# A planned attention and gated feed-forward kernel: a cast moved from GpSimd to ScalarE, a product from VectorE to GpSimd, and a new plan

## The chip, the cores and the metric

The kernel runs on one core of a Trainium2 chip. Its engines are TensorE (PE in the profile; PEld is its weight load), VectorE (DVE), ScalarE (ACT), GpSimd (POOL) and SyncE (SP, which here only issues DMAs). Each engine works through its own queue in order; semaphores tie the queues together. The metric is the device time of one execution in microseconds (us); less is better.

## The reference: what is computed

Linear attention with a sketched polynomial feature map, followed by a gated feed-forward layer. There are 4 batches of 4 heads, 1088 positions each, 32 dimensions per head, and r = 8, so that a position has 64 features.

```python
def phi(x):
    a = einsum('rd,bhsd->bhsr', S1, x)
    b = einsum('rd,bhsd->bhsr', S2, x)
    return einsum('bhsi,bhsj->bhsij', a, b)      # flattened to 64 features
q_p, k_p = phi(q), phi(k)
kv  = einsum('bhsf,bhsd->bhfd', k_p, v)
z   = sum(k_p, axis=2)
num = einsum('bhsf,bhfd->bhsd', q_p, kv)
den = einsum('bhsf,bhf->bhs', q_p, z)[..., None] + 1e-06
x   = (num / den)                                # to 4352 tokens x 128
out = (maximum(x @ w_gate, 0) * (x @ w_val)) @ w_out     # d_ff = 1536
```

## The kernel before, in words

**Tiling.** The 1088 positions of a head are laid out as 32 rows by 34 columns, four heads to 128 partitions. Columns 0 to 31 form groups of four, 128 tokens each (8 groups per batch); the last two columns of all batches are gathered into two more groups at the end. For the keys the 34 columns form nine groups of up to four (column 9a + x is in group x). An attention stage for the keys of a batch (class K) and one for the queries of a set of groups (classes Q and G) yield xT, 128 x tokens in fp16. Its consumer, class F, is a *unit* u: four blocks of 128 tokens times 128 hidden features (512 columns), in 103 units.

**Names of operations.** A unit has `g u` (gate product, L960, into a PSUM bank), `relu u` (ACT, L965, to a tile g_sb), `v u` (value product, L972), `h u` (DVE, L982: g_sb times the PSUM bank, to a tile ht; ten tiles ht are used in turn) or, for every sixth unit, `vcp u` and `hp u` (ACT copies the bank, L977, and POOL multiplies, L987), and `o u` (L994, the output product, which adds into the bank of its group; every `o` follows the `o` of the unit before). The last unit of a group has `oe` (ACT, L1002) and a store on SP (L1011). For the keys of batch b: `kt1` (transpose on DVE, L531), `ksk` (sketch, fp32 matmuls, L542), `kt2` (transpose from PSUM, L555), `z`, `zc`, `w`, `wc` (sums over positions for the denominator; L570, L578, L584, L588), `kphi b lo` (the feature products kp for groups lo onward, L599), `vc b h` (cast of half h of v from fp32 to fp16, L606), `kv` (L613) and `kve` (L620, to bz). For the queries: `qt1` (L1034), `qsk` (L735), `qt2` (L741), `bw`, `dn`, `rd`, `an` (denominator and quotient; L769, L776, L781, L801), `qphi` (features, L867), `qtr` and `qpt` (transpose on PE, L885, and copy to SBUF, L892) or `qtd` (a transposing DMA on SP, L875), `num` (L901) and `x` (to xT; L913, or L908 for the first two groups, which take a shorter way with `qaT`, `qc`, `rdx`, `rdT`). The weights arrive in fp32, in thirds `wg0` to `wo2`, and are cast by ACT (L426: wg0, wg1, wv1) or POOL (L428: wv0, wo0, wg2, wv2, wo1, wo2).

**The start.** All first loads go into SP's queue before anything else: k0 in two parts, q0 in two parts, v0 in four, then wg0, wv0, wg1, wv1, wo0, wg2, wv2, k1, wo1, wo2, q1. Until the first unit PE runs products of a zero tile (L330) that nobody reads, one stretch of them for each stretch in which the plan sees PE idle. For batch 0 the products `kv` run over head pair 0 first, which needs `vc 0 0`, then over head pair 1, which needs `vc 0 1`.

**What sets the order.** The program does not issue its operations as written. Each is put into a list with an engine, a modelled busy time and a modelled delay until others see its result (`busy + rec + LAT[engine]`), its inputs, the PSUM banks that it takes or gives up, and a due time. Due times of units are laid on a line (`T0 + u * U`, one unit every 0.65) and handed back from an operation to its inputs (`P.dues`). `P.run` then simulates the engines: it takes the operation that could start earliest, and among those of the same engine that could start within 0.2 of it (or half its own busy time, if that is less) the one with the earliest due time. Loads of the start have no queue in this model; a table `LAND` says when each has landed. The simulated start times are used for one thing alone: all operations are issued in their order, so that they fix the order of every engine's queue and of SP's loads and stores. On the chip an engine waits at the head of its queue for whatever is not ready.

`kphi 0 8`, the features of the ninth group of columns of batch 0, is on DVE before the change (list `own`), with a DVE transpose into a PSUM bank ahead of it (`kt2b`, L563), from which it reads one of its two factors. `vc 0 1` is on POOL; every other `vc` is on ACT.

Of the kernel before, what the change touches and what calls it, by code (L numbers as in the profile page):

```python
# [35 lines left out]
class Plan:  # L36


    HOLD = 2.0
    LAT = {"PE": 0.20, "DVE": 0.035, "ACT": 0.035, "POOL": 0.06, "SP": 0.0, "DMA": 0.05}  # L40

# [105 lines left out]
def kernel(  # L147
# [12 lines left out]
    nc = tc.nc  # L160

    B, H, S, D = q.shape
# [31 lines left out]
    wv = sb([DM, DF], FP16, "wv")  # L194
# [204 lines left out]
    def act(cols):  # L399
        return cols / 1200.0 + 0.062  # L400

    def pool(cols):
        return cols * 0.00188 + 0.07

    LAND = {"k0a": 3.6, "S": 4.3, "k0b": 4.25, "q0a": 5.4, "q0b": 7.35, "v0": 9.95, "wg0": 10.35,
            "wv0": 10.99, "wg1": 11.63, "wv1": 12.27, "wo0": 12.91, "wg2": 14.75, "wv2": 15.39,
            "k1": 16.75, "wo1": 17.39, "wo2": 18.03, "q1": 19.39}
    land = {n: P.landed(n, t) for n, t in LAND.items()}
# [43 lines left out]
    class K:  # L452


        def __init__(self, b, prev):
# [27 lines left out]
            self.lz = lz  # L483
            self.z_op = P.add("PE", f"z {b}", 0.40, self.z, self.t2s, take=[lz])
            self.zc_op = P.add("DVE", f"zc {b}", 0.12, self.zc, [self.z_op], drop=[lz], rec=0.07)
# [5 lines left out]
            cut = [(0, 2), (2, 4), (4, 6), (6, KX)] if b else [(0, 2), (2, 4), (4, 6), (6, 8), (8, KX)]  # L491
            own = [4] if b == 0 else []
            lb = Lease()
            self.lb = lb
            for n, (lo, hi) in enumerate(cut):
# [11 lines left out]
                else:  # L507
                    phis.append(P.add("POOL", f"kphi {b} {lo}", pool(cols),
                                      lambda lo=lo, hi=hi: self.phi(nc.gpsimd, lo, hi), dep))
            vc = [P.add(e, f"vc {b} {h}", 0.66 if e == "POOL" else 0.58,  # L510
                        lambda h=h, e=e: self.vc(h, e), [land[f"v{b}"]],
                        rec=0.0 if e == "POOL" else 0.13)
                  for h, e in enumerate(["ACT", "ACT" if b else "POOL"])]
            lm = Lease()
# [88 lines left out]

        def vc(self, h, e):
            o, i = (t[self.b][:, 2 * h:2 * h + 2] for t in (v16, v32))
            nc.scalar.copy(out=o, in_=i) if e == "ACT" else nc.gpsimd.tensor_copy(out=o, in_=i)  # L606

# [30 lines left out]
    class Q:  # L638
# [3 lines left out]
        def __init__(self, b, x0, n, i, ks, qt1, old):  # L642
# [26 lines left out]
            else:  # L669
                self.l4 = [Lease(2), Lease(2)]  # L670
                s1 = P.add("PE", f"qsk {name}", cols / 600.0 + 0.34 + 0.37 * (n > NX),
                           self.sk, qt1 + wcs + [wq_op], take=self.l4)
                t2, t2c = [P.add("DVE", f"qt2 {name} {i}", dve(2 * cols), lambda i=i: self.t2(i),
# [12 lines left out]
            if first:  # L686

                rx = P.add("ACT", f"rdx {name}", act(256), self.rdx, [o3], rec=0.13)
                lr = Lease()
                self.lr = lr  # L690
                rt = P.add("PE", f"rdT {name}", 0.52, self.rdT, [rx], take=[lr])
                self.rdc = P.add("ACT", f"rdTe {name}", act(256), self.rdTe, [rt], drop=[lr],
                                 rec=0.13)
                self.o4 = t2
            else:
                self.o4 = P.add(e, f"an {name}", small(x * R), lambda: self.div(eng), [o3] + old,
                                rec=0.07)
            self.t2_op = t2
# [216 lines left out]
    class F:  # L915


        def __init__(self, u, grp, qg, js, prev, old):
# [13 lines left out]
                      due=t + 0.35)  # L932
            vv = P.add("PE", f"v {u}", cost, self.v, [qg.x_op, wcast[f"wv{third}"]], take=[lv], rec=0.07,
                       due=t + 0.2)
            if self.pool:
                a2 = P.add("ACT", f"vcp {u}", act(cols), self.vcp, [vv], drop=[lv], rec=0.13,
                           due=t + 0.6)
# [165 lines left out]
    P.ops = order  # L1103
    P.dues(slack)
    end = P.run()
    if __name__ != "kernel":
# [44 lines left out]
```

## Time and profile before

| | |
|---|---|
| median of 3 runs | 100.52 us (100.48 to 100.69) |
| the profiled execution | 100.48 us |
| its span, first to last instruction | 98.7 us, 3036 instructions |
| busy: PE, PEld | 94.1 us (95%), 61.6 us (62%) |
| busy: DVE, ACT, POOL | 83.4 us (84%), 81.3 us (82%), 62.5 us (63%) |
| TensorE clock granted, mean | 0.996 of full |
| chain that ended last | PE 84%, DVE 6%, DMA 4%, issue 1%, SPq 1%, ACT 1% |
| first g of a unit starts | 13.20 us |

The profile shows one execution by the hardware profiler. A line of the timeline gives the start in us from the start of the span, the length, the engine, the line of the kernel and the instruction with its output and inputs; "x3" joins three that follow each other, and brackets hold the idle time of the engine before it and what ended it. Instructions of one engine overlap by some 0.1 us, so the next one may start before the length is over: where two follow without a gap, the distance of their starts is the price of one. Matmuls overlap more: 0.38 us for a matmul of 512 columns, and 0.216 from one start to the next. Waits that show on PEld (the weight load) may be covered by the matmuls that are still streaming.

### The profile page before, as it was taken

Reading aid. Unit: us, or ns where it says so; the run is one execution under the profiler, and the core shown is the slowest. Engines: PE = TensorE matmul, PEld = TensorE weight load, DVE = VectorE, ACT = ScalarE, POOL = GpSimd, SP = SyncE. Lnnn points to the kernel's source line nnn. Section 1 sums busy time; section 2 is a strip of 40 time slices with the busy share of each in tenths; the row PEclk is TensorE's granted clock in tenths of the full one; section 3 lists DMA queues with packets and bytes.
Section 4 is the critical chain, followed back from the end, with each engine's and each line's share of the span. In section 5 each row is a group of like instructions: output and inputs, shape, how many; then the busy total and the mean of one; then the engine's idle time right before and its main releaser. Section 6 shows DMA issues by size and latency. Waiting matters only on the chain.

```text
span 98.7 us, 3036 instructions
## 1 busy us (share of the span) xinstructions
PE 94.1 (95%) x1129; PEld 61.6 (62%) x1129; DVE 83.4 (84%) x180; ACT 81.3 (82%) x159; POOL 62.5 (63%) x68
## 2 busy tenths in 40 slices
PE   6999999999999999999999999999999999999960
PEld 2257678687475665565766665758566676668930
DVE  5979969999999998999999799976859687795960
ACT  3411979967999988999999489999899999989930
POOL 6159759999999897749949918698713404133000
PEclk9999999999999999999999999999999999999998
DMA  2999999478724289920435003004362300210041
GB/s 52 315 276 290 409 407 422 173 241 257 204 64 106 65 158 384 279 65 3 113 83 130 7 0 106 3 8 115 96 147 19 106 7 0 55 51 0 7 103 56
DMA packets 16784, 13.28 MB, mean 135 GB/s; under 512 B 8065, under 2 KB 14465, under 8 KB 16769
## 3 DMA queue, kind: packets, MB, share of 16 engines
q1 hardware_dynamic: 16736, 13.08, 45.4%
q8 instruction: 9, 0.15, 0.7%
q14 instruction: 7, 0.05, 0.2%
q10 hardware_dynamic: 32, 0.00, 0.0%
HBM read 9.14 MB, written 2.23 MB: 115 GB/s over the span
## 4 chain that ended last, share of the span: by engine, by line
PE 84%; DVE 6%; DMA 4%; issue 1%; SPq 1%; ACT 1%
PE ps L994 24%; PE ps L960 23%; PE ps L972 22%; DMA q_sb<-in_q_dram 4%; PE ps L901 4%; PE ps L735 2%; PE ps L542 2%; PE ps L613 2%; DVE qT L1034 1%; DVE qabc L741 1%; PE ps L885 1%; PE ps L570 1%; PE ps L746 1%; DVE ht L982 1%; DVE qqp L867 1%
## 5 line engine op out<-in xcount | busy, mean ns | idle before, releaser
L982 DVE TENSOR_TENSOR ht<-g_sb,ps 128x512 f16<-128x512 f16 (+1 forms) x87 | 55.4, 672 | 8.9 <-PE ps L972 4.1
L965 ACT ACTIVATE g_sb<-ps 128x512 f16<-128x512 f32 (+1 forms) x103 | 57.1, 612 | 5.8 <-PE ps L960 3.9
L960 PE MATMUL ps<-xT,wg 128*128 128x512 f16 (+1 forms) x120 | 39.0, 348 | 0.1
L994 PEld LDWEIGHTS <-ht 128*128 128x128 f16 x408 | 28.4, 98 | 16.9 <-POOL ht L987 3.6
L972 PE MATMUL ps<-xT,wv 128*128 128x512 f16 (+1 forms) x120 | 38.7, 348 | 0.0
L994 PE MATMUL ps<-wo,ht 128*128 128x128 f16 x408 | 37.0, 220 | 0.3 <-DVE ht L982 0.2
L987 POOL TENSOR_TENSOR ht<-g_sb,v_sb 128x512 f16<-128x512 f16 x16 | 18.6, 1165 | 16.8 <-ACT v_sb L977 12.3
L599 POOL TENSOR_TENSOR kp<-kab 128x512 f16<-128x512 f32 (+1 forms) x16 | 18.0, 1153 | 2.8 <-DVE kab L555 2.7
L867 POOL TENSOR_TENSOR qqp<-qan,qabc 128x1024 f16<-128x1024 f32 (+1 forms) x9 | 15.8, 1757 | 2.0 <-DVE qan L801 1.7
L972 PEld LDWEIGHTS <-wv 128*128 128x128 f16 x120 | 13.5, 115 | 3.3 <-issue 0.6
L960 PEld LDWEIGHTS <-wg 128*128 128x128 f16 x120 | 13.3, 114 | 3.1 <-issue 1.1
L977 ACT COPY v_sb<-ps 128x512 f32<-128x512 f32 x16 | 9.6, 600 | 0.0
L330 PE MATMUL ps<-zero 128*128 128x512 f16 (+5 forms) x23 | 6.7, 418 | 1.0 <-DVE maskkv L295 1.0
L1002 ACT ACTIVATE o_sb<-ps 128x512 f32<-128x512 f32 (+1 forms) x10 | 5.4, 543 | 1.5 <-PE ps L994 1.5
L1034 DVE STREAM_TRANSPOSE qT<-q_sb 128x576 f32<-128x576 f32 (+4 forms) x10 | 6.0, 610 | 0.4 <-DMA q_sb<-in_q_dram 0.4
L741 DVE STREAM_TRANSPOSE qabc<-ps 128x512 f32<-128x512 f32 (+2 forms) x8 | 5.4, 698 | 0.5 <-PE ps L735 0.5
L531 DVE STREAM_TRANSPOSE kT<-k_sb 128x544 f32<-128x544 f32 (+2 forms) x8 | 5.6, 724 | 0.0
L901 PE MATMUL ps<-qpt,bz 128*128 128x512 f16 (+2 forms) x26 | 5.3, 306 | 0.1
L913 ACT CAST xT<-ps 128x512 f16<-128x512 f32 (+1 forms) x9 | 5.0, 556 | 0.3 <-PE ps L901 0.3
L606 ACT CAST v<-v 128x576 f16<-128x576 f32 x7 | 4.6, 688 | 0.0
L330 PEld LDWEIGHTS <-zero 128*128 128x128 f16 x23 | 2.3, 117 | 3.0 <-issue 1.4
L613 PE MATMUL ps<-v,kp 128*128 128x64 f16 (+1 forms) x72 | 4.1, 193 | 0.0
(85 smaller groups left out, 63.0 us busy)
## 6 DMA issues: line engine op xcount, KB each, us to landing
v<-in_v_dram SPq DMA_DIRECT2D x15, 144.0 KB, 5.4
out_dram<-o_sb SPq DMA_DIRECT2D x28, 64.0 KB, 1.8
k_sb<-in_k_dram SPq DMA_DIRECT2D x3, 544.0 KB, 4.3
q_sb<-in_q_dram SPq DMA_DIRECT2D x3, 544.0 KB, 7.4
k_sb<-in_moe_w_out_dram SPq DMA_DIRECT2D x2, 256.0 KB, 4.8
q_sb<-in_q_dram SPq DMA_DIRECT2D x1, 416.0 KB, 5.5
k_sb<-in_k_dram SPq DMA_DIRECT2D x1, 288.0 KB, 2.8
k_sb<-in_k_dram SPq DMA_DIRECT2D x1, 256.0 KB, 3.0
```

The lines of the kernel that those rows point to most:

```text
L330: nc.tensor.matmul(PS[:, W_BANK, 0:m * w], zero, zero[:, None, 0:w].to_broadcast([128, m, w]), start=True, stop=True)
L599: eng.tensor_tensor(out=self.kp[:, lo:hi].rearrange("p x g (i a c) -> p (x g i) a c", i=2, a=R), in0=src[:, 0, :, :, None].to_broadcast([1 ...
L867: eng.tensor_tensor(out=self.qp[:, lo:hi].rearrange("p x g (i a c) -> p (x g i) a c", i=2, a=R), in0=a_in[:, :, :, None].to_broadcast([128 ...
L901: nc.tensor.matmul(o[:, 0:n * 128].rearrange("f (x t) -> f x t", x=n)[:, :, t], self.ks[b or 0].bz[:, p], self.pt[:, 0:n, p, t], start=(p ...
L960: nc.tensor.matmul(bank(self.lg)[:, y * W:(y + 1) * W], wblock(wg, j), x, start=True, stop=True, skip_group_check=True)
L965: nc.scalar.activation(out=self.gs[:, 0:self.cols], in_=bank(self.lg)[:, 0:self.cols], func=ACTF.Relu)
L972: nc.tensor.matmul(bank(self.lv)[:, y * W:(y + 1) * W], wblock(wv, j), x, start=True, stop=True, skip_group_check=True)
L977: nc.scalar.copy(out=self.vs, in_=bank(self.lv))
L982: nc.vector.tensor_tensor(out=self.ht[:, 0:w], in0=self.gs[:, 0:w], in1=bank(self.lv)[:, 0:w], op=ALU.mult)
L987: nc.gpsimd.tensor_tensor(out=self.ht, in0=self.gs, in1=self.vs, op=ALU.mult)
L994: nc.tensor.matmul(o[:, s], self.ht[:, y * W + s * 128:y * W + (s + 1) * 128], wo[:, j // 4, (j % 4) * DM:(j % 4 + 1) * DM], start=(j == 0 ...
L1034: nc.vector.transpose(qT[b][:, lo * 32:hi * 32], q_sb[b][:, lo * 32:hi * 32])
```

## The change

Five things change.

1. `vc 0 1` goes from POOL to ACT, so that both halves of v0 are cast there.
2. `own` becomes empty: `kphi 0 8` goes from DVE to POOL, and `kt2b` with its PSUM bank is not issued any more.
3. The table of landings gets other times; the order of the loads stays the same.
4. Modelled times change: PE's delay from 0.20 to 0.24, ACT's fixed part from 0.062 to 0.053, and the delays `rec` of `z`, `qsk`, `an` on POOL, `v` and `vcp`.
5. After the due times have been handed back, those of 78 operations are shifted by the amounts of a table, and not handed on to the operations before them.

Points 3 to 5 add and remove no operation; they change the order in which operations are issued. The diff, with its context cut:

```diff
@@ -37,7 +37,7 @@
-    LAT = {"PE": 0.20, "DVE": 0.035, "ACT": 0.035, "POOL": 0.06, "SP": 0.0, "DMA": 0.05}
+    LAT = {"PE": 0.24, "DVE": 0.035, "ACT": 0.035, "POOL": 0.06, "SP": 0.0, "DMA": 0.05}
@@ -397,14 +397,14 @@
     def act(cols):
-        return cols / 1200.0 + 0.062
+        return cols / 1200.0 + 0.053
-    LAND = {"k0a": 3.6, "S": 4.3, "k0b": 4.25, "q0a": 5.4, "q0b": 7.35, "v0": 9.95, "wg0": 10.35,
-            "wv0": 10.99, "wg1": 11.63, "wv1": 12.27, "wo0": 12.91, "wg2": 14.75, "wv2": 15.39,
-            "k1": 16.75, "wo1": 17.39, "wo2": 18.03, "q1": 19.39}
+    LAND = {"k0a": 3.6, "S": 4.3, "k0b": 4.25, "q0a": 5.4, "q0b": 7.3, "v0": 9.75, "wg0": 10.1,
+            "wv0": 10.74, "wg1": 11.38, "wv1": 12.02, "wo0": 12.66, "wg2": 13.3, "wv2": 14.94,
+            "k1": 16.3, "wo1": 16.94, "wo2": 17.58, "q1": 18.94}
@@ -481,7 +481,7 @@
-            self.z_op = P.add("PE", f"z {b}", 0.40, self.z, self.t2s, take=[lz])
+            self.z_op = P.add("PE", f"z {b}", 0.40, self.z, self.t2s, take=[lz], rec=-0.12)
@@ -489,7 +489,7 @@
             cut = [(0, 2), (2, 4), (4, 6), (6, KX)] if b else [(0, 2), (2, 4), (4, 6), (6, 8), (8, KX)]
-            own = [4] if b == 0 else []
+            own = [] if b == 0 else []
@@ -507,10 +507,8 @@
                     phis.append(P.add("POOL", f"kphi {b} {lo}", pool(cols),
-            vc = [P.add(e, f"vc {b} {h}", 0.66 if e == "POOL" else 0.58,
-                        lambda h=h, e=e: self.vc(h, e), [land[f"v{b}"]],
-                        rec=0.0 if e == "POOL" else 0.13)
-                  for h, e in enumerate(["ACT", "ACT" if b else "POOL"])]
+            vc = [P.add("ACT", f"vc {b} {h}", 0.58, lambda h=h: self.vc(h), [land[f"v{b}"]],
+                        rec=0.13) for h in range(2)]
@@ -601,9 +599,8 @@
-        def vc(self, h, e):
-            o, i = (t[self.b][:, 2 * h:2 * h + 2] for t in (v16, v32))
-            nc.scalar.copy(out=o, in_=i) if e == "ACT" else nc.gpsimd.tensor_copy(out=o, in_=i)
+        def vc(self, h):
+            nc.scalar.copy(out=v16[self.b][:, 2 * h:2 * h + 2], in_=v32[self.b][:, 2 * h:2 * h + 2])
@@ -669,7 +666,7 @@
-                           self.sk, qt1 + wcs + [wq_op], take=self.l4)
+                           self.sk, qt1 + wcs + [wq_op], take=self.l4, rec=-0.1)
                 t2, t2c = [P.add("DVE", f"qt2 {name} {i}", dve(2 * cols), lambda i=i: self.t2(i),
@@ -694,7 +691,7 @@
-                                rec=0.07)
+                                rec=-0.05 if e == "POOL" else 0.07)
@@ -930,10 +927,10 @@
             self.pool = u in pool_units
-            vv = P.add("PE", f"v {u}", cost, self.v, [qg.x_op, wcast[f"wv{third}"]], take=[lv], rec=0.07,
+            vv = P.add("PE", f"v {u}", cost, self.v, [qg.x_op, wcast[f"wv{third}"]], take=[lv], rec=0.03,
-                a2 = P.add("ACT", f"vcp {u}", act(cols), self.vcp, [vv], drop=[lv], rec=0.13,
+                a2 = P.add("ACT", f"vcp {u}", act(cols), self.vcp, [vv], drop=[lv], rec=0.17,
                 h = P.add("POOL", f"hp {u}", 1.13, self.hp, [a, a2, old], rec=0.06,
@@ -1102,6 +1099,29 @@
     P.dues(slack)
+
+
+    shift = {
+        "bw 2,0": -1.5, "dn 0,0": 5.1, "g 0": -1.3, "g 15": -0.5, "g 16": -0.5,
+        "g 18": -0.2, "g 20": -1.6, "g 25": -0.7, "g 28": -2.1, "g 30": 0.6,
+        "g 31": 0.8, "g 33": -2.1, "g 36": -0.3, "g 38": -0.4, "g 40": -1.0,
+        "g 42": -2.9, "g 43": -2.1, "g 9": -0.9, "h 13": 0.4, "h 19": 0.7,
+        "h 20": 3.2, "h 26": 1.5, "h 33": 2.8, "h 44": 3.9, "h 47": 6.5,
+        "h 6": -1.9, "ksk 0 1": -5.4, "kt1 2 1": 0.8, "kt2 0 2": 3.2,
+        "kt2 0 4": 1.9, "kv 1 2 0": -4.2, "kv 1 6 0": -0.5, "kv 2 0 0": 2.1,
+        "kve 2": -5.2, "num 2,0": -3.7, "o 13": 1.1, "o 15": 3.0, "o 19": -4.2,
+        "o 20": 0.9, "o 23": -4.3, "o 35": 12.8, "o 39": -7.4, "o 41": 2.6,
+        "o 43": 8.4, "o 46": 3.2, "o 48": -2.0, "o 49": 7.4, "o 9": 1.2,
+        "qaT 0,0": 2.4, "qphi 0,2": -1.9, "qpt 0,0": 0.5, "qsk 0,0 0": 5.2,
+        "qt1 2 16": 6.7, "qt1 3 0": 2.1, "qt2 3,0 1": -2.2, "v 10": -0.8,
+        "v 12": 0.7, "v 16": -0.6, "v 18": -0.6, "v 19": -1.0, "v 30": 1.1,
+        "v 31": -0.7, "v 33": -0.6, "v 34": -0.5, "v 35": 0.3, "v 36": 1.8,
+        "v 39": 1.6, "v 44": 1.1, "v 46": -1.2, "v 47": 1.0, "v 52": 0.5,
+        "v 53": -1.6, "v 54": 0.9, "w 0": -2.4, "w 1": 6.2, "wg0": 1.6,
+        "wv1": 1.9, "z 3": 1.1,
+    }
+    for o in P.ops:
+        o.due += shift.get(o.name, 0.0)
     end = P.run()
```

## The prediction

> **What bounds the kernel now.** I read the table of stretches first (busy time per engine in each stretch), because the means of the page (PE 95%, DVE 84%, ACT 82%) hide that the stretches have different limits. Columns: length, then busy time and instruction count of PE, weight load, DVE, ACT and POOL, then granted clock, DMA share and GB/s.
>
> ```profile
> 10.00:13.00 3.00, 2.85 (x45) 2.11 (x37) 2.96 (x9) 3.00 (x7) 1.76 (x3) 1.00 1.07 412
> 15.00:20.00 5.00, 4.90 (x65) 3.80 (x63) 4.75 (x8) 4.90 (x10) 5.00 (x7) 1.00 0.77 285
> 20.00:25.00 5.00, 5.00 (x93) 3.81 (x91) 5.00 (x11) 3.71 (x7) 4.93 (x5) 1.00 0.81 246
> 60.00:65.00 5.00, 5.00 (x47) 3.21 (x45) 4.14 (x8) 4.78 (x10) 3.64 (x4) 1.00 0.16 43
> 80.00:85.00 5.00, 5.00 (x49) 3.22 (x48) 3.87 (x7) 4.81 (x11) 1.17 (x1) 1.00 0.02 3
> ```
>
> From 60 us on only PE is full; from 15 to 25 POOL (5.00, 4.93 of 5) is as full as PE, and before 13 DVE and ACT are. Since a busy PE may still be waiting, I took the start times of successive matmuls in the trace and subtracted the spacing each kind has when fed (216 ns for 512 columns of L960, L972 and L901, 109 ns for 256, 55 ns for one L994, 28 ns for L613). Between the first L960 at 13.20 us and 94 us that leaves 7.0 us. Some 5 us sit inside or just behind the blocks of small fp32 matmuls (L542, L735, L570, L584), whose instructions the change keeps. Waits for an operand are the rest: at 14.40 us 0.12, 15.46 0.07, 16.80 0.24, 17.91 0.19, 24.82 0.07, 26.62 0.20, 27.44 0.08, 27.81 0.11 (together 1.06 before 28 us), then only 0.12 at 69.5 and 0.12 at 86.9. So the most that an order can win in the stream is about 1.3 us, nearly all before 28 us.
>
> Whom PE waits for there is read from the timeline, first of weight loads, then of POOL (start, length, instruction, in brackets the idle time before it and its releaser).
>
> ```profile
> 17.15 0.11 PEld L960 LDWEIGHTS <-wg 128*128 128x128 f16 x1 [0.23 <-issue]
> 18.20 0.45 PEld L885 LDWEIGHTS <-qqp 128*128 128x128 f16 x8 [0.28 <-POOL qqp L867]
> 27.03 0.76 PEld L994 LDWEIGHTS <-ht 128*128 128x128 f16 x12 [0.51 <-POOL ht L987]
> ```
>
> ```profile
> 10.54 0.66 POOL L606 CAST v<-v 128x576 f16<-128x576 f32 x1
> 11.14 0.61 POOL L428 CAST wv<-k_sb 128x512 f16<-128x512 f32 x1
> 13.49 1.07 POOL L867 TENSOR_TENSOR qqp<-qan,qabc 128x512 f16<-128x512 f32 x1 [1.74 <-DVE qan L801]
> 14.51 0.61 POOL L428 CAST wo<-k_sb 128x512 f16<-128x512 f32 x1
> 16.19 1.96 POOL L867 TENSOR_TENSOR qqp<-qan,qabc 128x1024 f16<-128x1024 f32 x1
> ```
>
> POOL stands idle for 1.74 us up to 13.49, then works with hardly a gap to 33 us, and PE's transposes at 18.20 start when POOL's features of query groups 4 to 7 end (16.19 + 1.96 = 18.15). The cast of wo0 at 14.51 could have run in the hole: its transfer landed at 12.89. That is the resource to watch.
>
> **The change part by part**, against the profiled execution's own 100.48 us (span 98.7 and 1.78 around it; the median of 100.52 lies 0.04 higher, which I leave alone).
>
> Second half of v0's cast, POOL to ACT. POOL loses 0.61 us (next cast 0.606 behind it). ACT gains 0.57, the spacing at which two such casts follow each other elsewhere. On ACT the first half starts at 10.08, so the second runs 10.65 to 11.32 instead of 10.54 to 11.20 on POOL: the second half of the kv products, which started at 11.25, starts 0.11 later, and the first unit with it (+0.11). Behind it on ACT move the copy of the transposed features, rdT and three weight casts, here with the hole that absorbs them:
>
> ```profile
> 10.66 0.58 ACT L892 COPY qpt<-ps 128x512 f16<-128x512 f16 x1
> 12.46 0.62 ACT L426 CAST wv<-q_sb 128x512 f16<-128x512 f32 x1
> 13.61 1.57 ACT L965 ACTIVATE g_sb<-ps 128x512 f16<-128x512 f32 x3 [0.53 <-PE ps L960]
> ```
>
> The feature copy would end at 11.81 (products use it at 12.22), rdT at 12.09 (used at 12.72), wg0 at 12.61 (first L960 at 13.20), wv1 at 13.65 against the first relu at 13.61. So 0.53 of the 0.57 is covered by ACT's wait, and 0.04 is not; without the cover it is 0.57. The shift of wv1's due time by +1.9 lets the relus pass it; its product is not due before 17.
>
> The ninth group of k0's features, DVE to POOL. DVE loses the transpose into PSUM (L563, 0.23) and the product (L599, 0.33 to its successor): 0.56. Little of it reaches the path: L at 7.29 waits for its own matmul, zs cannot start before the sums at 7.56 and a PE-to-DVE step of 0.21 (last kv matmul ends 11.68, bz starts 11.89), so 7.77 instead of 7.83, and the q transposes not before q0b's landing at 7.68 (now 7.93). I take 0.06 of a possible 0.2. POOL gains half of a 512-wide product, 1.03/2 = 0.51, up to 0.57 with a fixed part; against the cast it gave up, 0.04 to 0.10 less, so its wv0 cast stays near 11.1.
>
> Landings. The new table holds wg2 at 13.30 (old 14.75; landed 13.51), k1 at 16.30 (16.75; 16.23), q1 at 18.94 (19.39; 18.76): nearer. It has v0 at 9.75 (9.95; 10.01), wg0 to wo0 0.23 to 0.34 early: further off. Nothing is issued earlier, so no byte lands earlier; what it moves is the place of the casts. Taking wo0 into POOL's hole: 12.95 to 13.50, costing the features of query groups 2 and 3 up to 13.50 - 13.49 = 0.01 and freeing 0.57 from then on.
>
> One row speaks against all of the 0.57. The product L769 of 192 columns ran beside POOL's wv0 cast, the quotient L801 of the same size beside an idle POOL:
>
> ```profile
> 11.30 0.66 DVE L769 TENSOR_TENSOR bw<-qabc 128x192 f32<-128x192 f32 x1
> 13.06 0.35 DVE L801 TENSOR_TENSOR qan<-qabc,qrd 128x192 f32<-128x192 f32 x1
> ```
>
> 0.66 against 0.35, and the slow one ended 0.21 after POOL's cast (11.76). L801 would meet the wo0 cast in the same way: end at 13.50 + 0.21 = 13.71 instead of 13.41, so POOL's features would start 0.30 later and its lead from then on would be 0.57 - 0.30 = 0.27. The Trainium skill, page "SBUF — State Buffer", section "Who interferes with whom", says that a VectorE instruction with two SBUF inputs blocks against a GpSimd instruction that reads SBUF, whichever starts first; the two rows agree, and by that rule the sum takes the 0.27, without it the 0.57. From the rows alone the ends are 0.27 and 0.57; I take 0.27, since the pair of rows is of this very kind.
>
> Due times and the changed latencies. No work is added; 78 operations may change place on PE, DVE, ACT and POOL, and stores or transposing loads on SP behind them. The nearest rows for what an order is worth are the four waits at 24.8 to 27.8 us, 0.46 in all: between none of them gone and all; new ones of the same kind may come, so the lower end is -0.5 (longest row: 0.51, L994 for POOL's ht). I take half of the gain, 0.23. SP's queue is far from PE here: a transposing load takes 2.8 us to land and its result is needed later.
>
> Sum: first unit +0.11, but the same stream waits 0.24 and 0.19 at 16.8 and 17.9 for the POOL chain, which takes it up, so 0; POOL's lead -0.27; order -0.23; ACT's +0.04 and DVE's -0.06 cancel. 100.48 - 0.50 = 99.98, so 100.0.
>
> **Rivals.** (1) More: all 1.06 of the early waits go, and the late 0.12 + 0.12 too: 100.48 - 1.06 - 0.24 = 99.2. For: the waits are small and separate. Against: POOL is solid from 13.5 to 25, and an order does not shorten it. (2) No change: POOL still takes the features first, as it would if the quotient came just before wo0 landed, or the lead is spent at the next operand: 100.4. (3) Slower through ACT: the second v cast pushes relus instead of falling into the wait before 13.61. ACT is 4.90 of 5 busy from 15 to 20, so nothing gives it back: 100.48 + 0.57 = 101.05. It decides from the point where the three weight casts end later than about 13.6, that is, if v0 lands 0.1 us or more later than its 10.01. (4) Slower through the output products: o 35 is put off by 12.8 in due time. Every o follows the o before it, and a tile ht is reused ten units later, so products held back fill the ten tiles; PE then does a run of o while DVE gets nothing, and waits for the next ht. Price: the longest such wait, 0.51, so 101.0. It decides only if PE finds g and v to prefer for ten units; the stretches from 40 to 55 us (DVE 4.85, 5.00 and 4.47 of 5) speak against it, since DVE can fill ht hardly faster than it does now.
>
> **How the numbers follow.** Forecast 0.42 (its own range 99.6 to 100.3), more 0.15, no change 0.13, ACT 0.15, output products or another wait in their way 0.15. About 0.2% (0.2 us) is what a measurement of this kernel can tell from no change, so faster means under 100.3: 0.42 + 0.15 = 0.57; same 0.13; slower 0.30. The range from 99.2 to 101.0 reaches to rival 1 and to rival 4 and leaves out the ends beyond them.
>
> **What would show it.** Right: POOL's L428 of wo inside the hole before 13.5 and L867 of 1024 columns ending near 17.9 instead of 18.15; the 0.28 before L885 at 18 gone; eight L606 on ACT, the second at 10.65; no L563. The first L960 may lie at 13.3. Wrong: a first relu after 13.9 with ACT busy before it; a wait of more than 0.5 us before an L994 between 45 and 60; POOL's hole as long as now. The forecast fails if the new waits on PE beyond 28 us add up to more than 0.5 us, which nothing in the old trace shows, since the new order itself is not in it.

## The result and the profile after

The kernel after takes 102.06 us in the median (101.78 to 102.17); beside it the kernel before took 100.60 (100.48 to 100.90). The ratio is 1.0137, 95% interval 1.0099 to 1.0175: slower by 1.4%, where 100.0 was forecast. The profiled execution took 101.96 us, with a span of 100.2. All ratios here leave out executions more than 1.5% above the fastest of their kernel, and the traces of four runs below (the casts moved forward in the kernel before, its staging control, the second look at the kernel after, the last control) are of such executions, so that they show where a wait lies and not what the kernel takes.

The table of stretches of the kernel after (length, then busy time and instruction count of PE, weight load, DVE, ACT and POOL, granted clock, DMA share, GB/s) shows the place at once.

```profile
10.00:13.00 3.00, 2.89 (x36) 2.01 (x34) 2.80 (x9) 3.00 (x7) 2.12 (x4) 1.00 1.06 407
15.00:20.00 5.00, 4.70 (x74) 3.54 (x76) 4.81 (x9) 4.65 (x10) 4.38 (x5) 1.00 0.90 329
20.00:25.00 5.00, 4.93 (x92) 3.76 (x91) 4.93 (x11) 3.37 (x7) 4.80 (x6) 1.00 0.74 211
25.00:30.00 5.00, 3.69 (x44) 2.37 (x43) 3.55 (x8) 4.87 (x10) 3.35 (x4) 1.00 0.44 123
60.00:65.00 5.00, 5.00 (x47) 3.25 (x46) 4.62 (x10) 4.87 (x11) 3.51 (x4) 1.00 0.20 52
80.00:85.00 5.00, 5.00 (x47) 3.25 (x48) 3.80 (x7) 4.72 (x10) 1.17 (x1) 1.00 0.01 3
```

The same stretch of the kernel before, which the prediction did not show:

```profile
25.00:30.00 5.00, 4.96 (x59) 3.21 (x58) 4.92 (x10) 4.99 (x12) 4.75 (x6) 1.00 0.45 124
```

From 25 to 30 us PE is busy for 3.69 us instead of 4.96, and DVE and POOL lose 1.4 us each, while ACT stays full. So ACT is what the others wait for. The timeline of all engines around 25 us, kernel after (start, length, engine, line, instruction; in brackets the idle time before it and what ended it):

```profile
25.02 0.59 PE L969 MATMUL ps<-xT,wv 128*128 128x512 f16 x2
...
26.90 0.69 DVE L979 TENSOR_TENSOR ht<-g_sb,ps 128x512 f16<-128x512 f16 x1 [1.41 <-ACT g_sb L962]
26.92 0.38 PE L957 MATMUL ps<-xT,wg 128*128 128x512 f16 x1 [1.31 <-ACT g_sb L962]
26.92 0.42 PEld L991 LDWEIGHTS <-ht 128*128 128x128 f16 x4 [1.57 <-issue]
```

PE wants the next gate product (L957) and has no PSUM bank for it, since the relus that empty the banks (L962) have not run; DVE waits for the same relus. From start to start this one wait takes 1.47 us beyond the usual spacing, and the difference of the medians is 102.06 - 100.60 = 1.46. That the two agree to 0.01 is chance: of the 1.48 between the two profiled executions 1.11 arose up to the last matmul and 0.36 behind it (both are accounted for below). ACT's own timeline says why, first after, then before:

```profile
23.01 0.63 ACT L962 ACTIVATE g_sb<-ps 128x512 f16<-128x512 f32 x1
25.13 1.25 ACT L603 CAST v<-v 128x576 f16<-128x576 f32 x2 [1.49 <-DMA v<-in_v_dram]
26.28 2.54 ACT L962 ACTIVATE g_sb<-ps 128x512 f16<-128x512 f32 x5
```

```profile
23.74 2.37 ACT L965 ACTIVATE g_sb<-ps 128x512 f16<-128x512 f32 x4 [0.41 <-PE ps L960]
26.01 1.24 ACT L606 CAST v<-v 128x576 f16<-128x576 f32 x2
```

Before, four relus ran and then the casts of batch 1's values (`vc 1 0`, `vc 1 1`), with no wait. After, the same casts stand ahead of five relus, and v1 has not landed: ACT waits 1.49 us at the head of its queue, then casts for 1.25, and only then come the relus. The kernel's own plan put them there: its simulation has v1 landed at 23.24 and the first cast at 23.26, in a hole of ACT ahead of `relu 11`; in the kernel before it had 25.09 and 25.82. On the chip v1 landed after 24.6 in both (last recorded landing 24.93 before, 24.63 after, where the fourth load, the one that ended the wait, has no record). The plan moved its cast by 2.56 us for a landing that hardly moved.

Why the plan expected v1 earlier is seen on SP. v1's loads overwrite the tile through which the weight third wo2 came in, so they are issued behind POOL's cast of wo2; that cast went from 19.56 to 17.68 in the plan. On the chip it went from 19.77 to 17.83: 0.82 of it because POOL is ahead, the rest because it now runs ahead of a product `hp` and no longer behind it. In the plan this brings v1's issue so far forward that its model lets v1's transfer overtake that of k2, which SP issues first; with v1 held behind k2 the same plan has v1 at 24.84 (the run with a model that knows the queue), so 1.60 of the 1.85 us by which the plan's landing moved are that overtaking. SP's timeline, after, then before:

```profile
17.91 0.33 SPq L210 DMA_DIRECT2D k_sb<-in_k_dram  x1
18.47 2.94 SPq L216 DMA_DIRECT2D v<-in_v_dram  x4
```

```profile
18.73 0.33 SPq L210 DMA_DIRECT2D k_sb<-in_k_dram  x1
20.40 1.75 SPq L216 DMA_DIRECT2D v<-in_v_dram  x4
```

The first v1 load was issued 1.93 us earlier, as planned. But issuing the four took 2.94 us instead of 1.75 (the second alone 1.62), and they landed behind q2 (19.88) and k2 (23.73), which were still under way; nothing overtook.

### The profile page after: what moved, and what is told of

Its sections match the earlier page's. It is cut to its first block, busy times and chain, and to the rows that moved or that the text cites. A ratio compares the mean times of both kernels' runs of the same rounds, so it can differ in the third digit from the quotient of the medians.

```text
span 100.2 us, 3003 instructions
## 1 busy us (share of the span) xinstructions
PE 93.5 (93%) x1129; PEld 61.7 (62%) x1129; DVE 82.3 (82%) x178; ACT 81.1 (81%) x160; POOL 62.6 (63%) x68
## 4 chain that ended last, share of the span: by engine, by line
PE 67%; DMA 8%; DVE 7%; POOL 6%; SPq 4%; issue 3%; ACT 2%; ACTq 0%; DVEq 0%
PE ps L991 21%; PE ps L957 19%; PE ps L969 19%; DMA q_sb<-in_q_dram 5%; POOL qqp L864 3%; PE ps L898 3%; DMA v<-in_v_dram 3%; SPq L216 2%; PE ps L610 2%; PE ps L732 2%; POOL wo L428 2%; DVE ht L979 2%; PE ps L540 1%; DVE qT L1031 1%; DVE qabc L738 1%
## 5 line engine op out<-in xcount | busy, mean ns | idle before, releaser
L962 ACT ACTIVATE g_sb<-ps 128x512 f16<-128x512 f32 (+1 forms) x103 | 55.9, 607 | 5.1 <-PE ps L957 2.4
L957 PE MATMUL ps<-xT,wg 128*128 128x512 f16 (+1 forms) x120 | 36.8, 348 | 1.3 <-ACT g_sb L962 1.3
L969 PE MATMUL ps<-xT,wv 128*128 128x512 f16 (+1 forms) x120 | 37.1, 347 | 0.2 <-DVE ht L979 0.2
L991 PEld LDWEIGHTS <-ht 128*128 128x128 f16 x408 | 27.4, 98 | 13.5 <-issue 2.9
L991 PE MATMUL ps<-wo,ht 128*128 128x128 f16 x408 | 34.2, 219 | 0.2
L597 POOL TENSOR_TENSOR kp<-kab 128x512 f16<-128x512 f32 (+2 forms) x17 | 18.6, 1123 | 3.9 <-DVE kab L553 3.9
L957 PEld LDWEIGHTS <-wg 128*128 128x128 f16 x120 | 13.2, 115 | 5.8 <-issue 1.3
L969 PEld LDWEIGHTS <-wv 128*128 128x128 f16 x120 | 13.0, 113 | 4.3 <-issue 0.2
L330 PE MATMUL ps<-zero 128*128 128x512 f16 (+4 forms) x23 | 6.9, 425 | 1.0 <-DVE maskkv L295 1.0
L603 ACT CAST v<-v 128x576 f16<-128x576 f32 x8 | 5.1, 683 | 3.0 <-DMA v<-in_v_dram 3.0
L798 POOL TENSOR_TENSOR qan<-qabc,qrd 128x256 f32<-128x256 f32 (+1 forms) x3 | 2.0, 666 | 3.3 <-DVE qrd L778 3.3
```

The costliest lines, as they stand in the source:

```text
L330: nc.tensor.matmul(PS[:, W_BANK, 0:m * w], zero, zero[:, None, 0:w].to_broadcast([128, m, w]), start=True, stop=True)
L597: eng.tensor_tensor(out=self.kp[:, lo:hi].rearrange("p x g (i a c) -> p (x g i) a c", i=2, a=R), in0=src[:, 0, :, :, None].to_broadcast([1 ...
L957: nc.tensor.matmul(bank(self.lg)[:, y * W:(y + 1) * W], wblock(wg, j), x, start=True, stop=True, skip_group_check=True)
L962: nc.scalar.activation(out=self.gs[:, 0:self.cols], in_=bank(self.lg)[:, 0:self.cols], func=ACTF.Relu)
L969: nc.tensor.matmul(bank(self.lv)[:, y * W:(y + 1) * W], wblock(wv, j), x, start=True, stop=True, skip_group_check=True)
L991: nc.tensor.matmul(o[:, s], self.ht[:, y * W + s * 128:y * W + (s + 1) * 128], wo[:, j // 4, (j % 4) * DM:(j % 4 + 1) * DM], start=(j == 0 ...
```

## The experiments

Ratios are to the kernel before on the same chip, with 95% intervals. Theory A is the wait of ACT for v1; its rivals are named where they are tested. A figure used beside the ratios is the *stream*: the time from the first gate product to the last matmul of a profiled execution, 82.19 us before and 83.24 after.

**Casts behind relu 11 to 13.** In the kernel after, the two casts are issued three relus later, about where the kernel before has them.

```diff
+    late = ['vc 1 0', 'vc 1 1']
+    moved = [o for o in todo if o.name in late]
+    todo = [o for o in todo if o.name not in late]
+    at = 1 + next(i for i, o in enumerate(todo) if o.name == 'relu 13')
+    todo[at:at] = moved
```

> The changed kernel with one move in ScalarE's queue: the two casts of v1 go behind the next three relus (11 to 13); every other queue is as in the changed kernel. Theory A (ScalarE stands at the head of its queue for the landing of v1, PE runs out of free banks for 1.47 us): the idle time of 1.49 us before the casts of v1 and the wait of 1.31 us before a gate product go; 102.06 - 1.47 = 100.6, between 100.3 and 100.9. Theory B (the loss is the extra cast of v0 on ScalarE, rival 3 of the prediction) and theory C (the loss is spread over many small waits made by the due times): 101.8 to 102.2.

Measured: ratio 1.0126 (1.0044 to 1.0209), profiled execution 101.29 us. The casts no longer wait, but little is won. ACT's timeline and the table of waits from 24 to 29 us:

```profile
24.49 1.77 ACT L962 ACTIVATE g_sb<-ps 128x512 f16<-128x512 f32 x3 [0.73 <-DVE qabc L738]
26.15 1.24 ACT L603 CAST v<-v 128x576 f16<-128x576 f32 x2
27.29 1.10 ACT L962 ACTIVATE g_sb<-ps 128x512 f16<-128x512 f32 x2
```

```profile
PEld L610 <- issue: 1.2, 1, 1.2
PE ps L610 <- ACT g_sb L962: 0.9, 1, 0.9
```

The hole that the plan meant for the casts (0.73 in front of 24.49) now stays empty, 1.25 us of casts fall into the stretch where ACT has no slack, and PE, whose order is unchanged, comes to the kv products of batch 1 (L610) before their time and waits there 0.9 us for a relu behind the casts. A miss for theory A's number. With the rest of the order written for early casts, moving them alone moves the wait.

**v1 ahead of k2.** SP issues v1's loads before k2's.

```diff
+    late = ['k2 issue']
+    ...
+    at = 1 + next(i for i, o in enumerate(todo) if o.name == 'v1 issue')
```

> The changed kernel with one move in SyncE's queue: the four loads of v1 are issued ahead of the load of k2, as the plan's model of the transfers had it; every other queue is as in the changed kernel, the casts of v1 stay where they were. Theory A, with the landing of v1 as its cause: v1 lands near 23 us instead of near 25, ScalarE's idle time before its casts falls under 0.4 us, and the time is 100.3 to 100.9. Theories B and C: no change, 101.8 to 102.2.

Measured: 1.0042 (0.9993 to 1.0091), profiled execution 101.32 us. v1's recorded landings are 21.26, 22.48 and 24.70, and the casts still wait until 24.77:

```profile
22.87 0.63 ACT L962 ACTIVATE g_sb<-ps 128x512 f16<-128x512 f32 x1
24.77 1.25 ACT L603 CAST v<-v 128x576 f16<-128x576 f32 x2 [1.28 <-issue]
```

So k2's place ahead is not what keeps v1 from landing at 23.2: with k2 issued behind (21.35), the four loads of 144 KB still take from q2's landing (19.66) to 24.70. What the wait is worth this run can't say: the profiled execution has it almost in full (PE loses 1.25 us in front of that gate product, and the stream is 83.13) and is shorter than that of the kernel after by an earlier first unit (13.03 against 13.27) and a shorter end (3.29 us behind the last matmul against 3.67). The fastest executions (100.17, 100.52) have no trace.

**The same fault in the kernel before.** There the casts are moved ahead of relu 10 to 13.

```diff
+    late = ['vc 1 0', 'vc 1 1']
+    ...
+    at = 1 + next(i for i, o in enumerate(todo) if o.name == 'vcp 10')
```

> The kernel before with one move in ScalarE's queue: the two casts of v1 go ahead of the relus 10 to 13, to the place that they have in the changed kernel. Theory A: ScalarE waits there for the landing of v1 at about 25 us, PE loses 1.0 to 1.5 us: 101.6 to 102.1. Theories B and C: 100.4 to 100.8, since neither the cast of v0 nor a due time is touched.

Measured: 1.031 (1.0204 to 1.0416), more than expected. Two lines of its timelines, ACT's and PE's:

```profile
25.74 1.24 ACT L606 CAST v<-v 128x576 f16<-128x576 f32 x2 [2.21 <-DMA v<-in_v_dram]
```

```profile
27.53 0.59 PE L972 MATMUL ps<-xT,wv 128*128 128x256 f16 x2 [2.79 <-ACT g_sb L965]
```

Nothing else of the change is in this kernel, and a wait of the same kind costs it 2 to 4% (the interval rests on two executions). A cast whose operand is late, ahead of relus, is enough for a loss of this size. It is larger than expected for two reasons: the wait is 2.95 us instead of 1.0 to 1.5, and the granted clock (the third figure from the end in the table of stretches) falls with it:

```profile
28.00:30.00 2.00, 2.00 (x6) 0.65 (x5) 1.75 (x4) 1.16 (x2) 0.99 (x2) 0.50 0.00 1
```

Behind the wait the clock is 0.50 for this stretch, and matmuls of 512 columns start 0.43 us apart instead of 0.216; in the kernel after, behind its 1.47, it stays 1.00. Three of the four executions have a mean clock of 0.980 and took 104.3 to 104.9 us, the fourth has 1.000 and took 102.96. So in the traced execution the longer wait was paid for twice: at half clock from some 27.5 to 30.7 us, half of those 3.2 us, 1.6, is an estimate of the second price.

**No shift of due times.**

```diff
-        o.due += shift.get(o.name, 0.0)
+        pass
```

> The changed kernel without the table of shifts, all else as in the change (landings, model times, the cast of v0 on ScalarE, the features on GpSimd). Its plan puts the casts of v1 behind two more relus. Theory A: at most 0.3 us of the wait is left, 100.4 to 101.0. Theory B: the extra cast is still there, 101.8 to 102.2. Theory C: the due times are gone, 100.4 to 100.8.

Measured: 1.0041 (1.0008 to 1.0074), profiled execution 101.0 us. Without the table the plan keeps the casts late, one at a time between relus, and they do not wait:

```profile
26.02 0.68 ACT L603 CAST v<-v 128x576 f16<-128x576 f32 x1
26.59 0.61 ACT L962 ACTIVATE g_sb<-ps 128x512 f16<-128x512 f32 x1
27.08 0.68 ACT L603 CAST v<-v 128x576 f16<-128x576 f32 x1
```

So of the five parts of the change the table of shifts, on top of the other four, brings the long wait. The belief about v1 is not enough for it: this plan, too, has v1 landed at 23.24, and still puts the first cast at 25.21. Theory A and theory C expected nearly the same time here, so the run does not separate them. In return this kernel waits 0.57 us twice earlier (at 14.7 and 16.6), so it is not the kernel before either.

**v1 early.** wo2 gets a staging tile of its own, so that v1's loads need not wait for its cast, and they are issued before q2's.

```diff
-           [half(k_sb[2], 0), half(k_sb[2], 1), half(v1, 0)]]
+           [half(k_sb[2], 0), half(k_sb[2], 1), sb([128, W3], FP32, "wo2_st")]]
...
+    late = ['v1 issue']
+    ...
+    at = next(i for i, o in enumerate(todo) if o.name == 'q2 issue')
```

> The changed kernel, in which wo2 is staged in a tile of its own instead of in v1's, so that v1's four loads need no cast before them and are issued ahead of q2's load, at about 12 us instead of 18.5; every other queue is as in the changed kernel. Theory A (the casts of v1 on ScalarE and the products with it on PE stand in their queues for the landing of v1 at about 25 us): v1 lands before 23.5, ScalarE's idle time before its casts is under 0.4 us, no wait of PE over 0.6 us is left, and the time is 100.3 to 100.9. Theories B (the extra cast of v0 on ScalarE) and C (many small waits made by the due times): 101.8 to 102.2.

Measured: 1.0027 (0.9981 to 1.0073), over executions that scatter from 99.91 to 102.76; the profiled one is the fastest, 99.91 us with a span of 98.1.

```profile
23.71 1.27 ACT L603 CAST v<-v 128x576 f16<-128x576 f32 x2
24.85 2.58 ACT L962 ACTIVATE g_sb<-ps 128x512 f16<-128x512 f32 x5
```

Three of v1's loads landed at 20.18, 20.85 and 21.55 (the fourth has no record), the casts start behind the relu without a wait, and PE's wait is gone: the stream is 81.28 us, 0.9 less than before. But this is the fastest of twelve, and the median of all of them is 101.40, so the run shows what the new order can do with v1 early, not what it does. q1 now lands at 19.74, 0.11 us before DVE takes it (19.85); that this thin margin makes the scatter is argued, not shown.

**The control for it.** The same staging and issue order in the kernel before.

> The kernel before with wo2 staged in a tile of its own and v1's loads issued ahead of q2's: the control of the run with the same edit on the changed kernel. Nothing waits for v1 in the kernel before, so all theories: no change, 100.4 to 100.8.

Measured: 1.0184 (1.0123 to 1.0246), where no change was expected. Now k2 is the late one, behind v1 and q2, and DVE stands for it (DVE's timeline):

```profile
26.10 0.74 DVE L531 STREAM_TRANSPOSE kT<-k_sb 128x544 f32<-128x544 f32 x1 [2.38 <-DMA k_sb<-in_k_dram]
```

So it is no control, since its edit makes a wait of its own, but it shows the mechanism on another engine: in this execution PE then loses 2.31 us, and the granted clock from 28 to 30 us is 0.50 as above. An order is tuned to the landings that it was made with, and earlier for one load is later for another.

**Casts later and the kv products later too.** The casts behind relu 12, and three of the four parts of batch 1's kv products behind `g 17`, to clear the wait that the first run had left.

```diff
+    for late, mark in ((["vc 1 0", "vc 1 1"], "relu 12"),
+                       (["kv 1 0 0", "kv 1 2 0", "kv 1 4 0"], "g 17")):
+        ...
```

> The changed kernel with two moves: on ScalarE the casts of v1 go behind relu 11 and 12, on PE the first three parts of the products with v1 go behind the gate product of unit 17, some 1.2 us of work further on; v1 lands as late as before. Theory A: both waits (1.3 us before a gate product, 1.07 us before the products with v1 when only the casts were moved) shrink to 0.3 us together: 100.5 to 101.0. Theories B and C: 101.6 to 102.2.

Measured: 1.013 (1.008 to 1.0179): a miss. The wait went on to the value products, 0.80 us at 27.04, and to two of 0.32 and 0.25 behind it. ACT had no slack there for casts that come late.

**v0's second cast back on POOL.** The prediction's third rival put a loss on ScalarE's second cast of v0. In the kernel after, only that cast goes back.

```diff
-            nc.scalar.copy(out=v16[self.b][:, 2 * h:2 * h + 2], in_=v32[self.b][:, 2 * h:2 * h + 2])
+            o, i = (t[self.b][:, 2 * h:2 * h + 2] for t in (v16, v32))
+            if self.b == 0 and h == 1:
+                nc.gpsimd.tensor_copy(out=o, in_=i)
+            else:
+                nc.scalar.copy(out=o, in_=i)
```

> The changed kernel with the second half of v0 cast by GpSimd again, at the place in the order that the plan gives it; the rest of every queue is as in the changed kernel. GpSimd does it behind its fifth feature product, so it ends near 11.7 instead of 11.1 us and the first unit starts up to 0.5 us later; the wait for v1 is untouched. Theory A: 101.7 to 102.5. Theory B (the extra cast on ScalarE is the loss): 100.6 to 101.5. Theory C: 101.8 to 102.2.

Measured: 1.0197 (1.0143 to 1.0251). The wait for v1 is untouched, and the first unit starts at 14.04 instead of 13.27:

```profile
25.97 1.25 ACT L607 CAST v<-v 128x576 f16<-128x576 f32 x2 [1.43 <-DMA v<-in_v_dram]
```

So the rival falls: with the rest of the new plan, the move of that cast is no loss. (On POOL it now stands behind a fifth features product that was not there before the change, so this does not price the move by itself.)

**The kernel after once more**, as a base for the last runs.

> The changed kernel once more, unchanged, so that it stands beside the next runs on the same chip. All theories: 101.8 to 102.3, with the wait of about 1.4 us before a gate product near 25 us.

Measured: 1.0154 (1.0116 to 1.0191), which agrees with 1.0137.

**A model that knows the queue.** The planner is told that v1's transfer starts after k2's, and plans afresh.

```diff
+    land["v1"].after.append(land["k2"])
+    land["k2"].succ.append(land["v1"])
```

> The changed kernel with one wrong belief of the plan mended: its model lets the transfer of v1 start only after that of k2, so that v1 is believed to land at 24.8 instead of 23.2 us; the landings on the chip, the table of shifts and all else stay, and the order is planned anew. Theory A (the loss is made by planning the casts of v1 for a landing that comes 1.8 us later): the casts are planned behind relu 11 to 13, no wait for v1 over 0.4 us is left, 100.5 to 101.3. Theory C (the shifted due times by themselves): 101.8 to 102.2.

Measured: 1.0106 (1.0061 to 1.0151), a miss for theory A's number. The plan now has the casts at 25.87, behind relu 11 to 13, and on the chip they run without a wait:

```profile
26.41 1.81 ACT L965 ACTIVATE g_sb<-ps 128x512 f16<-128x512 f32 x3 [0.73 <-DVE qabc L741]
28.10 1.25 ACT L606 CAST v<-v 128x576 f16<-128x576 f32 x2
```

It is still slower than before. In its profiled execution the stream is 82.16 us, as short as before, and the loss lies ahead of it: the first unit starts at 15.46, as the second part of q0 landed at 8.40 instead of 7.38 and the granted clock from 10 to 15.5 us was 0.69. Whether the other executions lose their time there too is not known.

**v1 in the stage of wo0.** An attempt to free v1's tile early by staging wo0 in it and wo2 in k2's tile.

> The changed kernel, in which v1's tile stages wo0 and k2's tile wo2 (exchanged), so that v1's loads wait only for wo0's cast and are issued at about 14.3 us, ahead of q2's load; no tile is added, and every other queue is as in the changed kernel. Theory A: v1 lands before 23.5, the wait for it is gone as with the separate tile (span 98.1 there, against 100.2), q1 is delayed less than there, since v1's packets come later: 99.7 to 100.7. Theory C: 101.8 to 102.2.

Its edit issued v1's loads ahead of the cast of wo0 from that tile, so that cast waited for v1, and a third of w_out was made of v1's numbers: 1.0914 (1.0865 to 1.0962). It tells nothing of the question.

**The exchange done rightly, landings as measured, and a fresh search for shifts.**

The loads are also chained in the order v1, q2, k2 (not shown in the diff).

```diff
-           [half(k_sb[2], 0), half(k_sb[2], 1), half(v1, 0)]]
+           [half(v1, 0), half(k_sb[2], 1), half(k_sb[2], 0)]]
...
+        land[n].start = land[n].done = t
...
-    shift = {
+    shift = {'L|DVE': -2.843,
...
```

> The previous kernel with the plan told where v1, q2, k2 and v2 land with these stagings (22.6, 24.0, 26.4, 28.7 us) and with another table of shifts, tuned on that model. Theory A (orders that fit the landings carry over to the chip): 99.0 to 100.2, below both kernels. Theory C (shifted due times make small waits whatever the landings): 100.8 to 102.2.

Measured: 1.0154 (1.0111 to 1.0198). The wait for v1 is gone (first cast at 23.19), but others came, the longest again for a landing, that of a transposing DMA (timeline at 53 us):

```profile
53.32 0.60 PE L905 MATMUL ps<-qpt,bz 128*128 128x512 f16 x2 [1.37 <-DMA qpt<-qqp]
```

The planner ended this plan at 95.33 us, the plan after at 96.40, the plan before at 97.13. On the chip the kernel before is the fastest of the three.

**The wait alone.** All runs so far that removed the wait moved something else as well. Here the casts of batch 1 read the tile of v0, which landed before 10 us. Every instruction, size and order is that of the kernel after, and v1 is still loaded.

```diff
-            nc.scalar.copy(out=v16[self.b][:, 2 * h:2 * h + 2], in_=v32[self.b][:, 2 * h:2 * h + 2])
+            nc.scalar.copy(out=v16[self.b][:, 2 * h:2 * h + 2], in_=v32[0 if self.b == 1 else self.b][:, 2 * h:2 * h + 2])
```

> The kernel after, with one thing changed: the two casts of batch 1's values read the fp32 tile of v0, which landed before 10 us, and no longer the tile of v1. Same instructions, same sizes, same order on every engine, same loads; only ScalarE's wait for v1's landing goes. (Batch 1's kv products are then made of v0's numbers, so a quarter of the output isn't the reference's.) Theory A, the wait of ScalarE for v1 at the head of its queue is the whole loss: casts at about 23.3 without a wait, no wait of PE above 0.4 us between 24 and 28, and the time falls by about the 1.47 us of that wait, to 100.4 to 101.0, a ratio to the kernel before of 0.998 to 1.004. Rival B, the loss sits in the rest of the plan and the wait only shows it first: PE waits as long a few units later, and the time stays above 101.5, ratio above 1.009.

Measured: 0.998 (0.995 to 1.0009); median 100.83, and 100.71 for the kernel before beside it. ACT's timeline and the stretch:

```profile
23.80 0.63 ACT L962 ACTIVATE g_sb<-ps 128x512 f16<-128x512 f32 x1
24.29 1.27 ACT L603 CAST v<-v 128x576 f16<-128x576 f32 x2
25.43 2.58 ACT L962 ACTIVATE g_sb<-ps 128x512 f16<-128x512 f32 x5
```

```profile
25.00:30.00 5.00, 5.00 (x56) 3.44 (x55) 4.96 (x11) 4.98 (x11) 4.65 (x5) 1.00 0.45 124
```

The casts follow the relu at once and PE is full from 25 to 30 us, though v1's last recorded load landed at 24.95 here, so that a cast of v1 would have stood from 24.29 until then at least. The loss went with the one wait, and rival B falls. The stream is 82.15 us, against 82.19 before and 83.24 after. (In this execution PE lost some 0.5 us more from 13 to 25 than in that of the kernel after, mostly in two waits of 0.38 and 0.57 at 15.2 and 16.9, and its first unit came 0.27 later, so it ends no earlier than the kernel before.)

**Its control.** The same operand in the kernel before, where the casts had nothing to wait for.

> Control for the run above: the kernel before, with the casts of batch 1 reading v0's tile in the same way. There v1 had landed when its casts came up, so nothing waited for it but some 0.07 us at 24.8. Theory A: no change, ratio 0.998 to 1.002 (100.3 to 100.8). If the time falls by more than 0.3 us, reading a tile that no transfer touches is worth something by itself, and the run above has to be read less that amount.

Measured: 0.9978 (0.9951 to 1.0005), no change that can be told. The two ratios differ by 0.0002, each within some 0.3%: without the one wait the kernel after is as fast as the kernel before, and of the 0.5 us that was forecast for the rest nothing shows (up to some 0.4 could hide in the two intervals).

## Why the prediction was wrong, step by step

**The step that failed** is the term for due times and latencies, -0.23 us with a lower end of -0.5. It priced an order by the waits in the old trace (longest 0.51), and the new order made one of 1.47. The sentence "SP's queue is far from PE here" was wrong: ACT's cast waits for the v1 loads in SP's queue, the cast was ahead of the relus, and PE takes a bank from each relu. It looked at the transposing loads alone.

**The step on landings** led to it. "Nothing is issued earlier, so no byte lands earlier; what it moves is the place of the casts" was said of the loads of the start. For v1, whose issue hangs on POOL's cast of wo2, the plan's landing did move, by 1.85 us, set off by the prediction's own "resource to watch", POOL's lead: it let v1's transfer overtake k2's in the plan, though not on the chip. The belief and the shifts were both needed, since the plan without shifts leaves the casts at 25.21 and the plan with v1 behind k2 has them at 25.87. The prediction followed that lead forward to PE and not to the loads that wait for POOL's casts to free their stages. In the old trace they stand at 20.40, right behind that cast.

**POOL's lead** was real and larger than its 0.27. POOL's timeline of the kernel after, and two rows of DVE's:

```profile
11.06 0.74 POOL L428 CAST wv<-k_sb 128x512 f16<-128x512 f32 x1
12.68 1.07 POOL L864 TENSOR_TENSOR qqp<-qan,qabc 128x512 f16<-128x512 f32 x1 [0.88 <-DVE qan L798]
13.69 0.61 POOL L428 CAST wo<-k_sb 128x512 f16<-128x512 f32 x1
...
14.82 1.95 POOL L864 TENSOR_TENSOR qqp<-qan,qabc 128x1024 f16<-128x1024 f32 x1
```

```profile
10.95 0.38 DVE L766 TENSOR_TENSOR bw<-qabc 128x192 f32<-128x192 f32 x1
...
12.24 0.36 DVE L798 TENSOR_TENSOR qan<-qabc,qrd 128x192 f32<-128x192 f32 x1
```

The second features product ended at 16.77 against 18.15, 1.38 us earlier: 0.82 is the lead, the rest comes from wv2's cast, which now runs behind the product and not ahead of it. The way was another than forecast: wo0's cast did not go into the hole but behind the first product, and the hole shrank from 1.74 to 0.88 because the quotient came 0.82 earlier. So the argued slowdown of the quotient beside a cast did not arise. The product beside POOL's wv0 cast took 0.38 this time, and the cast 0.74 instead of 0.61. The Trainium skill ("SBUF — State Buffer", section "Who interferes with whom") says that a VectorE instruction with two SBUF inputs contends with a GpSimd instruction that reads SBUF, and that issue order decides who blocks. Here DVE began first (10.95 against 11.06) and POOL was the one that lost, where in the kernel before it was DVE. The rows agree with it.

**Where the gain went.** The lead did not reach the end. PE came to the query transposes earlier but with fewer feed-forward products done (at 18 us 3.25 us of product time against 3.90), and waited 0.46 there. By the prediction's method of spacings, now with one table of spacings for both kernels (which puts the old total at 7.36 instead of 7.0), PE lost 2.49 us from 13 to 25 before and 2.28 after; from 25 to 30 it lost 0.43 and 1.64; from 30 to 94 4.44 and 4.49. So before 25 us the new plan won 0.21 of the 0.50 forecast (0.1 to 0.2 by other choices of the spacings), the stretch with the wait cost 1.21, and beyond 30 us the new order was worth nothing (0.05 lost). With the 0.07 of the later start this is 1.12, and the last matmul is 1.11 later (96.50 against 95.39). (The eight early waits of the prediction add up to 1.08, not 1.06; nothing hangs on it.)

**The start** came when it was forecast, though in part by luck. ACT's timeline after:

```profile
9.87 1.25 ACT L603 CAST v<-v 128x576 f16<-128x576 f32 x2 [1.50 <-DMA v<-in_v_dram]
11.02 0.40 ACT L781 COPY rdx<-qrd 128x256 f32<-128x256 f32 x1
11.33 0.57 ACT L889 COPY qpt<-ps 128x512 f16<-128x512 f16 x1
...
12.32 0.37 ACT L791 COPY rdT<-ps 128x256 f32<-128x256 f32 x1
...
13.71 1.09 ACT L962 ACTIVATE g_sb<-ps 128x512 f16<-128x512 f32 x2
```

The first unit starts at 13.27 (forecast 13.31), the first relu at 13.71 (13.65): the hole before the first relu took the cast, as said. But the second half of the kv products, which was to delay the first unit, was not late at all (11.24, before 11.25), since v0 landed 0.21 us earlier than in the old trace. What delayed it is the copy rdT, which ended at 12.69, right ahead of the product for x that needs it (12.73): ACT now does the copy before it in that chain, rdx, behind both casts (11.02 instead of 9.69). The rival that saw the cast push the relus is refuted by its return to POOL (1.0197), and by the run without the wait, which keeps the cast on ACT and loses nothing.

**The rivals.** The slower one through `o 35` and the tiles ht did not happen: no gap of PE over 0.35 us lies between 45 and 60 us. The prediction had the class "another wait in their way" with 0.15 and its upper end 101.0 at a wait of 0.51; the case that came is of that class, at three times the price. Its test "new waits on PE beyond 28 us" looked just past the place.

## What to carry to other kernels

An operation put at the head of an in-order queue for a landing bets everything behind it on that landing: price it by the work queued behind and by the landing's own uncertainty, not by the waits of the old trace. A wait that takes the granted clock down with it, as in the casts moved forward, costs more than its length. When an engine gets faster, follow what its ends release, the stages and the loads behind them too, and ask which consumers the plan will then move forward. A planner's end is no forecast where it hugs modelled landings: here plans of 97.13, 96.40 and 95.33 us gave ratios of 1, 1.014 and 1.015.

## What the runs showed of the hardware

Issuing a load on SP usually takes 0.3 to 0.45 us here, but 1.62 when q2 and k2 were still under way (18.85, after) and 1.65 in the run with v1 first (18.70, q2 under way). At the end one store of the kernel after took 2.11 us to issue (of the 3.44 for four):

```profile
93.94 3.44 SPq L1008 DMA_DIRECT2D out_dram<-o_sb  x4
97.48 0.38 SPq L1013 DMA_DIRECT2D out_dram<-o_sb  x1
```

In the kernel before the same four took 1.78 (92.83 to 94.61), and the last store did not wait for them. From the last matmul to the end of the span this makes 3.67 us after against 3.31 before, 0.36 of the 1.48 by which the two profiled executions differ; in the run without the wait the long issue was there too (1.96); in the one without shifts it was not (0.44), nor in the one with v1 first (0.43). Why it comes is open.

In the run with v1 ahead of k2, v1's four loads of 144 KB took 5.0 us from q2's landing on (19.66 to 24.70), where the kernel's model has 2.90; issued ahead of q2, in the run with v1 early, three of them landed 0.67 and 0.70 us apart (20.18, 20.85, 21.55). What slows them in the first case isn't settled.

The granted clock stayed 1.00 behind PE's wait of 1.47 us (kernel after, 26 to 30 us) and of 1.25 (v1 first). Behind waits of 2.31 and 2.95 us (the staging control and the casts moved forward, both in the kernel before) it was 0.50 from 28 to 30 us and back at 1.00 from 32 on. Where between them the change lies no run shows.
